# A shorter last chunk ahead of the branch, and a re-planned order of mirrored loads

## The chip, the cores and the metric

The kernel runs on one core of a Trainium2 chip. The time is device microseconds of one execution; the number that counts is the median over several runs.

## The reference

Three networks in a row, in single precision:

```python
# attention without softmax; u, v: (4, 3072, 256), z: (4, 3072, 64)
scores = (1 / S) * np.matmul(z, z.transpose(0, 2, 1))
x = (u * np.matmul(np.maximum(scores, 0.0) ** 2, v)).reshape(B * S, D)
# mixture of 8 experts with 384 slots each; x[i] goes to expert argmax(x[i] @ w_gate)
# in the order of i while that expert has slots left; later tokens are dropped
h = np.maximum(np.einsum('ecd,edf->ecf', disp, w1), 0.0)   # (8, 384, 1024)
y = np.einsum('ecf,efd->ecd', h, w2)                       # (8, 384, 256)
out[i] = gate_w[i] * y[expert_idx[i], pos[i]]   # gate_w: softmax weight; 0 where dropped
# feed-forward with ELU: 256 -> 2048 -> 256; w_in and w_out are float64
result = elu(out @ w_in) @ w_out
```

Only tokens that got a slot have an output that isn't zero. Once all 8 x 384 slots are full, the attention of all later tokens is not needed.

## The kernel before, in words

**Stages.** The kernel computes the attention of the first 3456 tokens (all of batch 0 and 384 queries of batch 1), then reads the count of the least used expert (`need`) and branches. If every expert has its 384 slots full, it goes on to the experts at once (`experts(FIRST)`); else it computes further chunks of queries until they are (`attention("later")`, not executed with these inputs). The experts run one after another, each with its 16 steps of the feed-forward network interleaved with the preparation of the next expert, with an order written out by hand (`feed_forward`).

**Attention.** The queries are cut into chunks: six of 512 (chunks 0 to 5, batch 0) and one of 384 (chunk 6, batch 1). A chunk has 24 steps, one for each tile of 128 keys. A plain step has a score (two matmuls of 128 keys by the chunk's queries, L620), a ReLU and a square on ScalarE (L1085, L1091), a rounded part (the cast, on ScalarE at L113 or VectorE at L923), the remainder on VectorE (L116), and the attend (six matmuls, L124 to L127). So numbers of single precision go through TensorE as a rounded part and a remainder, in three products.

**Mirrored steps.** Scores of batch 0 are symmetric. Where a later chunk needs a block that an earlier one computed, the earlier one stores it to DRAM (`m_store`, L653), and the later one loads it (`m_load`, four DMAs, L659) and transposes it on VectorE (L1072), in place of score, ReLU and square. `MC` says for how many tiles of each pair (row of keys, chunk) this is done: 39 steps, in chunks 1 to 5.

**Routing.** After a chunk's last attend, `route` multiplies by u (the gates, L694), forms tokens as rows with the logits beside them (matmuls, L708; copies, L720 and L722), and computes expert, position and gate weight with some 25 small VectorE operations. Then each tile of 128 tokens is scaled (L895 or L897) and scattered to `disp` in DRAM by an indirect DMA that GpSimd issues (L903). The order of the experts is set from the counts after chunk 5 (`first_expert`): the fullest one is the first, its weights are loaded, and once chunk 5 is scattered its rows are loaded (SP, L162), transposed on TensorE (L217) and split. The routing of chunk 6 itself (`trail`) runs beside the first expert.

**The order of the work.** A planner at build time (`Conductor`) places the instructions of the attention stage on TensorE, ScalarE, VectorE and SP, with modelled durations. TensorE's scores and attends have a fixed order (items). Every other job has an item for which it is needed and a `tail`, how long before it; the job whose due time is earliest goes first. A `gate` holds a job back until an item is reached; `after` names what it waits for, with extra time if given as a pair. On SP, the planner counts a backlog of DMA traffic (`dma`). The plan is then run as it is: each engine's queue is in order.

**Buffers.** The squares and the mirrored blocks live in 11 plain buffers (`own`); rounded parts and remainders in 7 (`ownr`) and in ten that are borrowed from the second network's weights until chunk 6.

**Other work in the stage.** `narrowing` turns the float64 weights into pairs of single precision on VectorE: eight loads of 1 MB, one every 14 steps from step 8 on. `fills` writes zeros to the output. `keys` and `values` load and split z and v.

## Time and profile before

| what | value |
|---|---|
| runs shown | 724.52, 725.9 and 1425.81 us, median 725.9 |
| the profiled execution | 723.64 us, its span 721.4 us |
| TensorE busy | 706.7 us of the span |
| VectorE, ScalarE busy | 569.5 us, 575.6 us |
| attention stage, to the first matmul of the first expert | 0 to 304.25 us |
| mean granted TensorE clock | 0.997 |

The times of the table are those of the chip; a row of the profile is from one execution. In what follows, TensorE is PE (its weight loads PEld), VectorE is DVE, ScalarE is ACT, GpSimd is POOL, and SP is the engine that issues most DMAs (SPq its queue). L620 is line 620 of the kernel before. The span begins at the first instruction.

### The profile page before, as it was taken

What the parts mean: (1) busy time and instruction counts of PE and PEld (TensorE: products, weight loads), DVE (VectorE), ACT (ScalarE), POOL (GpSimd) and SP (SyncE); (2) the same over time, 40 slices, a digit from 0 to 9 for tenths busy, and PEclk for the clock granted to TensorE, in tenths of its full rate; (3) what the DMA queues carried; (4) which work ended last, traced back from release to release, by engine and by line L of the source; (5) the groups of instructions that cost most, each with busy time, mean ns of one, the idle gap of its engine ahead of it and who ended that gap; (6) DMA issues with size and microseconds to landing.
All of it is one profiled execution on the core that took longest, in us unless ns stands there. A gap on an engine that the chain in (4) does not pass through costs nothing. (4 is left out here: it accounts for less than half of the span.)

```text
span 721.4 us, 11551 instructions
## 1 busy us (share of the span) xinstructions
PE 706.7 (98%) x3756; PEld 638.2 (88%) x3756; DVE 569.5 (79%) x1217; ACT 575.6 (80%) x1191; POOL 67.9 (9%) x108
## 2 busy tenths in 40 slices
PE   8999999999999999999999999999999999999996
PEld 5888888887888889998989999999999999999995
DVE  7879799788997989678867777777777777787782
ACT  7999988887897899749767777777787777787891
POOL 1003200220002200220001001001001001001011
PEclk9999999999999999999999999999999999999998
DMA  6967968799888969638440600801704405200000
GB/s 167 269 199 204 244 148 192 174 202 221 175 145 211 187 200 282 240 125 246 177 126 16 205 8 23 225 1 35 215 1 127 122 8 167 97 1 22 1 23 22
DMA packets 197856, 98.36 MB, mean 136 GB/s; under 512 B 145894, under 2 KB 188428, under 8 KB 197280
## 3 DMA queue, kind: packets, MB, share of 16 engines
q1 hardware_dynamic: 195344, 91.10, 48.3%
q0 software_dynamic: 2448, 6.49, 2.5%
q8 instruction: 30, 0.49, 0.3%
q14 instruction: 34, 0.28, 0.1%
HBM read 58.37 MB, written 38.10 MB: 134 GB/s over the span
## 5 line engine op out<-in xcount | busy, mean ns | idle before, releaser
L1689 PE MATMUL o<-wout,gh 128*128 128x512 f32 x384 | 139.3, 394 | 0.0
L1664 DVE SCALAR_TENSOR_TENSOR t<-x,t 128x384 f32<-128x384 f32 x128 | 71.4, 558 | 83.8 <-ACT t L1661 82.5
L1659 ACT ACTIVATE m<-h 128x384 f32<-128x384 f32 x128 | 62.7, 490 | 68.6 <-PE h L127 68.3
L1693 PE MATMUL o<-wout,gl 128*128 128x256 f32 x384 | 107.2, 280 | 0.2 <-DVE gl L116 0.2
L1085 ACT ACTIVATE own<-s 128x512 f32<-128x512 f32 (+1 forms) x129 | 73.3, 569 | 24.8 <-PE s L620 22.4
L124 PE MATMUL h<-xh,win 128*128 128x384 f32 x256 | 86.2, 337 | 0.5 <-DVE g L1667 0.3
L125 PE MATMUL h<-xh,win 128*128 128x384 f32 x256 | 85.6, 334 | 0.0
L1689 PEld LDWEIGHTS o<-wout,gh 128*128 128x128 f32 x384 | 71.9, 188 | 11.1
L1091 ACT ACTIVATE own<-own 128x512 f32<-128x512 f32 (+1 forms) x129 | 78.4, 609 | 2.4
L1667 DVE SCALAR_TENSOR_TENSOR g<-h,t 128x384 f32<-128x384 f32 x128 | 71.3, 557 | 4.4
L1693 PEld LDWEIGHTS o<-wout,gl 128*128 128x128 f32 x384 | 72.7, 189 | 1.1 <-DVE gl L116 0.9
L1660 ACT ACTIVATE x<-m 128x384 f32<-128x384 f32 x128 | 67.3, 525 | 4.1
L116 DVE TENSOR_TENSOR gl<-g,gh 128x384 fp32r<-128x384 f32 x128 | 70.0, 547 | 0.2 <-ACT gh L113 0.2
L113 ACT ACTIVATE gh<-g 128x384 fp32r<-128x384 f32 x128 | 65.3, 510 | 1.0 <-DVE g L1667 0.9
L127 PE MATMUL h<-xl,win 128*128 128x384 f32 x256 | 65.7, 337 | 0.0
L1661 ACT ACTIVATE t<-m 128x384 f32<-128x384 f32 x128 | 65.1, 508 | 0.0
L127 PE MATMUL acc<-ownr,vs 128*128 128x512 f32 (+1 forms) x198 | 58.5, 377 | 0.0
L124 PE MATMUL acc<-ownr,vs 128*128 128x512 f32 (+1 forms) x154 | 57.7, 375 | 0.0
L125 PE MATMUL acc<-ownr,vs 128*128 128x512 f32 (+1 forms) x154 | 57.4, 372 | 0.0
L124 PEld LDWEIGHTS h<-xh,win 128*128 128x128 f32 x256 | 48.0, 188 | 6.3 <-DVE g L1667 1.2
L620 PE MATMUL s<-zs 128*128 128x512 f32 (+1 forms) x129 | 50.3, 390 | 0.2 <-ACT row L722 0.2
L1708 POOL DMA_INDIRECT out_dram<-oy,toks x21 | 21.5, 1024 | 296.8 <-DVE oy L1707 265.5
(152 smaller groups left out, 1685.9 us busy)
## 6 DMA issues: line engine op xcount, KB each, us to landing
raw<-in_moe_w_dram SPq DMA_DIRECT2D x16, 1024.0 KB, 6.4
out_dram<-fill SPq DMA_DIRECT2D x32, 384.0 KB, 6.5
own<-mir SPq DMA_DIRECT2D x156, 64.0 KB, 2.9
vr<-in_v_dram SPq DMA_DIRECT2D x24, 256.0 KB, 3.6
mir<-own SPq DMA_DIRECT2D x28, 192.0 KB, 2.5
raw<-in_moe_w_in_dram SPq DMA_DIRECT2D x4, 1024.0 KB, 5.6
raw<-in_moe_w_out_dram SPq DMA_DIRECT2D x4, 1024.0 KB, 7.6
win<-win_d SPq DMA_DIRECT2D x8, 512.0 KB, 4.6
```

The lines of the kernel that those rows point to most:

```text
L113: nc.scalar.activation(out=out, in_=src, func=func)
L116: nc.vector.tensor_tensor(out=out, in0=src, in1=fp(hi), op=ALU.subtract)
L124: nc.tensor.matmul(out=ps, lhsT=hi, rhs=rh, start=first, stop=False)
L125: nc.tensor.matmul(out=ps, lhsT=lo, rhs=rh, start=False, stop=False)
L127: nc.tensor.matmul(out=ps, lhsT=hi, rhs=rl, start=False, stop=last)
L1085: nc.scalar.activation(out=s["a"][:, :nq], in_=s.pop("ps"), func=ACTF.Relu)
L1091: nc.scalar.activation(out=a, in_=a, func=ACTF.Square)
L1660: nc.scalar.activation(out=self.x, in_=self.m, func=ACTF.Exp, scale=-1.0)
L1664: nc.vector.scalar_tensor_tensor(out=self.t, in0=self.x, scalar=1.0, in1=self.t, op0=ALU.add, op1=ALU.mult)
L1667: nc.vector.scalar_tensor_tensor(out=self.g, in0=self.ps, scalar=0.0, in1=self.t, op0=ALU.max, op1=ALU.add)
L1689: both = lambda: nc.tensor.matmul(out=o, lhsT=hi[:, sl], rhs=w.rearrange("p a d -> p (a d)"), start=(f == 0), stop=(f == NF2 - 1),)
L1693: one = lambda: nc.tensor.matmul(out=o[:, 0:D], lhsT=lo[:, sl], rhs=w[:, 0, :], start=False, stop=False)
```

## The change

- The last chunk ahead of the branch has 320 queries (`QB`), not 384. Of its three tiles of tokens the last has 64 rows (`part`); the rows left over are zeroed. 384 stays the size of later chunks and of the zero fills (`QC`). With these inputs the least used expert, which has 384 slots, gets 386 of the first 3392 tokens (393 of the first 3456).
- Two mirrored steps fewer (`MC`): 37, not 39.
- Planner: a mirrored load may be placed 20 items ahead (17 before) and is due 11 us before its use (8 before); its transpose is planned 2.5 us after the load, that of u 2 us after its load; jobs on SP that are needed for an item are held back while the planned backlog is over 4 us.
- Narrowing starts a load every 11 steps, not 14.
- The assumed arrival of loads at the start is 7.6 and 9.1 us for the third and fourth key load (7.2 and 8.2 before) and 8.5 us for the fourth value load (8.2 before).

```diff
-    QA, QB = 512, 384
+    QA, QB, QC = 512, 320, 384
...
-            if e == "SP" and x.need is None:
-                t = max(t, self.dma - 0.5)
+            if e == "SP":
+                t = max(t, self.dma - (0.5 if x.need is None else 4.0))
...
-    FIRST, NZ = S + QB, QB
+    FIRST, NZ = S + QB, QC
+    NZERO = -(-FIRST // NZ)
...
-        MC = {(0, 1): 3, (0, 2): 4, (1, 2): 3, (0, 3): 3, (1, 3): 3, (2, 3): 3, (0, 4): 3, (1, 4): 3, (2, 4): 2, (3, 4): 2, (0, 5): 2, (1, 5): 2, (2, 5): 2, (3, 5): 2, (4, 5): 2}
+        MC = {(0, 1): 3, (0, 2): 4, (1, 2): 3, (0, 3): 3, (1, 3): 3, (2, 3): 2, (0, 4): 3, (1, 4): 2, (2, 4): 2, (3, 4): 2, (0, 5): 2, (1, 5): 2, (2, 5): 2, (3, 5): 2, (4, 5): 2}
...
-            n = nq // P
-            t0 = (b * S + q0) // P
+            n, t0 = -(-nq // P), b * S + q0
+            part = [min(P, nq - j * P) for j in range(n)]
...
+                        if part[-1] < P:
+                            nc.gpsimd.memset(t["row"][part[-1]:P, n - 1, :], 0.0)
...
+            if part[-1] < P:
+                chain("oh", lambda: nc.vector.memset(t["oh"][part[-1]:P, n - 1, :], 0.0))
...
-            LEAD, AHEAD = (3 if more else 2), 17
+            LEAD, AHEAD = (3 if more else 2), 20
...
-                        "SP", 4 * sync(nq), None, need=a_item, tail=8.0, gate=max(0, a_item - AHEAD),
+                        "SP", 4 * sync(nq), None, need=a_item, tail=11.0, gate=max(0, a_item - AHEAD),
...
-                    before(w, load)
+                    before(w, (load, 2.5))
...
-                    b, 0, {g: Begun(5.2 + g, zr=zl[g]) for g in (2, 3)},
+                    b, 0, {g: Begun(4.6 + 1.5 * g, zr=zl[g]) for g in (2, 3)},
...
-                values(b, 0, {n: Begun((5.0, 5.9, 6.8, 8.2)[n], vr=vl[n]) for n in range(4)}, {})
+                values(b, 0, {n: Begun((5.0, 5.9, 6.8, 8.5)[n], vr=vl[n]) for n in range(4)}, {})
...
-                    t = add("DVE", dve_turn(nq), None, after=[x], need=end, tail=0.9)
+                    t = add("DVE", dve_turn(nq), None, after=[(x, 2.0)], need=end, tail=0.9)
...
-            W, EVERY = 512, 14
+            W, EVERY = 512, 11
...
-            for i in range(FIRST // NZ):
+            for i in range(NZERO):
```

The rest of the diff cuts operands of the last tile to 64 rows and adapts the chunks after the branch.

## Rows read from the trace of the kernel before

**Rows 1.** The page: busy us of each engine, share of the span, instructions.
```profile
PE 706.7 (98%) x3756; PEld 638.2 (88%) x3756; DVE 569.5 (79%) x1217; ACT 575.6 (80%) x1191; POOL 67.9 (9%) x108
```

**Rows 2.** Waits, whole span: engine, line, what it waited for: total us, times, longest.
```profile
DVE own L1072 <- DMA own<-mir: 2.6, 4, 0.7
...
PE acc L127 <- DVE win L116: 0.9, 3, 0.4
```

**Rows 3.** Timeline, TensorE: start us, us, engine, line; steps in chunks 3 and 6.
```profile
149.98 0.39 PE L620 MATMUL s<-zs 128*128 128x512 f32 x1
151.80 0.39 PE L620 MATMUL s<-zs 128*128 128x512 f32 x1
...
285.85 0.33 PE L620 MATMUL s<-zs 128*128 128x384 f32 x1
...
287.24 0.33 PE L620 MATMUL s<-zs 128*128 128x384 f32 x1
```

**Rows 4.** Timeline, TensorE and its weight loads, near the end.
```profile
713.36 0.42 PEld L1693 LDWEIGHTS o<-wout,gl 128*128 128x128 f32 x2
713.59 0.40 PE L1693 MATMUL o<-wout,gl 128*128 128x256 f32 x2
...
713.82 0.39 PE L1689 MATMUL o<-wout,gh 128*128 128x512 f32 x1
```

**Rows 5.** Busy us in stretches: us, each engine (instructions), granted clock, DMA share, GB/s.
```profile
140.00:180.00 40.00, 39.08 (x179) 31.56 (x179) 34.85 (x79) 31.69 (x59) 5.06 (x9) 1.00 0.88 201
...
268.30:290.90 22.60, 22.60 (x141) 22.41 (x140) 20.69 (x69) 21.23 (x48) 0.79 (x5) 1.00 0.95 286
290.90:301.40 10.50, 10.02 (x58) 9.70 (x56) 7.88 (x16) 9.17 (x20) 4.47 (x4) 1.00 0.67 224
```

**Rows 6.** Groups by shape, whole span: count, busy us, mean ns, idle before.
```profile
L1091 ACT ACTIVATE own<-own 128x512 f32<-128x512 f32 x105 | 65.9, 629 | 1.9
...
L1091 ACT ACTIVATE own<-own 128x384 f32<-128x384 f32 x24 | 12.5, 522 | 0.5
...
L116 DVE TENSOR_TENSOR ownr<-own,ownr 128x512 fp32r<-128x512 f32 x28 | 19.2, 685 | 4.5 <-ACT ownr L113 4.3
...
L116 DVE TENSOR_TENSOR ownr<-own,ownr 128x384 fp32r<-128x384 f32 x24 | 13.3, 556 | 3.6 <-ACT ownr L113 2.1 <-ACT row L722 0.7
```

**Rows 7.** The same view, VectorE, 268.3 to 290.9: remainders and casts of chunk 6.
```profile
L116 DVE TENSOR_TENSOR ownr<-own,ownr 128x384 fp32r<-128x384 f32 x14 | 7.7, 553 | 0.9 <-ACT row L722 0.7
...
L923 DVE CAST ownr<-own 128x384 fp32r<-128x384 f32 x7 | 2.5, 359 | 0.3 <-ACT own L1091 0.2
```

**Rows 8.** Timelines of four engines: from chunk 5's gates to the first expert.
```profile
268.36 0.68 DVE L694 SCALAR_TENSOR_TENSOR ur<-acc,ur 128x512 f32<-128x512 f32 x1
...
290.66 1.34 POOL L903 DMA_INDIRECT disp<-row,idx  x1 [16.28 <-DVE row L897]
...
297.66 0.37 SPq L162 DMA_DIRECT2D rows<-disp  x1
...
301.43 0.87 PE L217 MATMUL dps<-ident,rows 128*128 128x128 f32 x6 [0.51 <-DMA rows<-disp]
...
304.25 0.34 PE L124 MATMUL h<-dh,w1hl 128*128 128x384 f32 x1
```

**Rows 9.** Timelines of TensorE and VectorE at the start.
```profile
8.86 0.50 PE L571 MATMUL zps<-identr,t 128*128 128x128 f32 x4 [1.03 <-DVE t L116]
...
9.28 0.29 DVE L1149 CAST t<-zr 128x256 fp32r<-128x256 f32 x1 [0.56 <-DMA zr<-in_z_dram]
9.49 0.68 DVE L116 TENSOR_TENSOR ownr<-own,ownr 128x512 fp32r<-128x512 f32 x1
```

**Rows 10.** The page, DMA issues: queue, count, KB each, median us to landing.
```profile
own<-mir SPq DMA_DIRECT2D x156, 64.0 KB, 2.9
```

More of the change, by code (lines that the diff above doesn't have):

```diff
@@ L59, in tile_attn_moe_ffn @@
     CT = cap // P
-    QA, QB = 512, 384
-    assert D == 256 and E == 8 and DQ == 64 and cap % P == 0 and S % QA == 0 and S % QB == 0
+    QA, QB, QC = 512, 320, 384
+    assert D == 256 and E == 8 and DQ == 64 and cap % P == 0 and S % QA == 0
     cscale = (1.0 / S) ** 2
@@ L708, in turn_x @@
                         nc.tensor.matmul(
-                            out=t["xps", j][:, d * RH:(d + 1) * RH],
-                            lhsT=us[c][:, d, j * P:(j + 1) * P], rhs=iw[:, d, :],
+                            out=t["xps", j][0:part[j], d * RH:(d + 1) * RH],
+                            lhsT=us[c][:, d, j * P:j * P + part[j]], rhs=iw[:, d, :],
                             start=True, stop=True,
@@ L717, in copy @@
                 def copy(j=j, by_dve=by_dve):
-                    ps = t.pop(("xps", j))
+                    ps, to = t.pop(("xps", j))[0:part[j], :], t["row"][0:part[j], j, :]
                     if by_dve:
-                        nc.vector.tensor_copy(out=t["row"][:, j, :], in_=ps)
+                        nc.vector.tensor_copy(out=to, in_=ps)
                     else:
-                        nc.scalar.activation(out=t["row"][:, j, :], in_=ps, func=ACTF.Copy)
+                        nc.scalar.activation(out=to, in_=ps, func=ACTF.Copy)
                 y = put("copy", "DVE" if by_dve else "ACT", 0.36, [x], 8, cost=1.0)(copy)
@@ L891, in scaled @@
                 def scaled(j=j):
-                    row, g = t["row"], t["g"]
-                    r = row[:, j, 0:TOK]
+                    q = part[j]
+                    row, g = t["row"][0:q, j, :], t["g"][0:q, j, :]
+                    r, at = row[:, 0:TOK], row[:, TOK:TOK + 1].bitcast(I32)
                     if scales[j].ran == "ACT":
-                        nc.scalar.activation(out=r, in_=r, func=ACTF.Copy, scale=g[:, j, :])
+                        nc.scalar.activation(out=r, in_=r, func=ACTF.Copy, scale=g)
                     else:
                         nc.vector.tensor_scalar(
-                            out=r, in0=r, scalar1=g[:, j, :], scalar2=None, op0=ALU.mult
+                            out=r, in0=r, scalar1=g, scalar2=None, op0=ALU.mult
                         )
-                    nc.gpsimd.tensor_copy(
-                        out=row[:, j, TOK:TOK + 1].bitcast(I32), in_=tok[:, t0 + j:t0 + j + 1]
-                    )
+                    if t0 % P:
+                        nc.gpsimd.iota(at, pattern=[[0, 1]], base=t0 + j * P, channel_multiplier=1)
+                    else:
+                        nc.gpsimd.tensor_copy(out=at, in_=tok[0:q, t0 // P + j:t0 // P + j + 1])
                     put = nc.gpsimd.indirect_dma_start(
                         out=disp[:, :],
-                        out_offset=bass.IndirectOffsetOnAxis(ap=t["idx"][:, j, :], axis=0),
-                        in_=row[:, j, :],
+                        out_offset=bass.IndirectOffsetOnAxis(ap=t["idx"][0:q, j, :], axis=0),
+                        in_=row,
                         in_offset=None,
@@ L1561, in first_flow @@
                         ps = layer1(0, f)
-                        go_on((QB // P, 2, 0)[f] if f < 3 else 1)
+                        go_on((-(-QB // P), 2, 0)[f] if f < 3 else 1)
                         hidden(0, f, ps)
@@ L1598, in later_flow @@
         def later_flow():
-            later = [(b, q, QB) for b in range(1, B) for q in range(0, S, QB)][1:]
+            odd = (S - QB) % QC + QC
+            later = [(1, QB, odd)] + [
+                (b, q, QC) for b in range(1, B) for q in range((QB + odd) * (b == 1), S, QC)
+            ]
+            assert odd <= QA and odd % SQ == 0
             with ExitStack() as ifs:
@@ L1747, in feed_forward @@
             for z in range(4):
-                i = reach // NZ + 4 * (n - 1) + z
+                i = -(-reach // NZ) + 4 * (n - 1) + z
                 if i < NTOK // NZ:
@@ L1829, in tile_attn_moe_ffn @@
     with tc.If(told[0] > 0, preferred_fallthrough_block=True, label="usual") as seldom:
-        for i in range(FIRST // NZ, NTOK // NZ):
+        for i in range(NZERO, NTOK // NZ):
             zero(i)
```

## The prediction

> **What bounds the kernel now.** I read the busy times of the page first. TensorE is busy nearly all of the span, VectorE and ScalarE about four fifths each [rows 1]. So time is either TensorE's work or one of its few gaps, and I went on to the waits for those gaps [rows 2], then to the timeline for what one step costs [rows 3, 4], and last to the stretch this change is about, the last chunk ahead of the branch, "chunk 6" (batch 1, 384 queries, 24 steps). It runs from the gates of chunk 5 at 268.4 to the first matmul of the first expert at 304.25 [rows 8]. The table of windows shows what an average over the span hides: in 268.3 to 290.9 TensorE is busy throughout, but so are ScalarE (21.2 of 22.6 us) and VectorE (20.7 of 22.6) [rows 5]. Three engines are full there at once.
>
> There is a second thing to see in that stretch. The first expert's rows are gathered from what chunk 5 routed. The chain is: gates of chunk 5 (268.36), routing on VectorE in small pieces, four indirect stores on GpSimd (first at 290.66), the load of the rows on SP (297.66), transposes on TensorE (301.43, after an idle 0.51), then the expert's first layer (304.25) [rows 8]. At 301.43 TensorE had already waited for the rows, and it had only two attend steps left. So two paths end together: TensorE's own work, and the routing chain of chunk 5. Only the first gets shorter with fewer queries.
>
> **The change part by part.**
>
> *Fewer queries.* A step of 512 queries takes 151.80 - 149.98 = 1.82 us, one of 384 takes 287.24 - 285.85 = 1.39 us [rows 3]. Both have eight matmuls, so 128 columns are worth 0.43 us a step and 64 columns 0.215. Over 24 steps TensorE saves 24 x 0.215 = 5.2 us. The three 128-row tiles of routing become two and a half, with the same instructions.
>
> Could a matmul of 320 columns be held up by its weight load? The matmul would have 0.147 us, a recorded weight load lasts 0.19, and TensorE's load row is full in chunk 6 (22.4 of 22.6 us) [rows 5]. But at the end two matmuls of 256 columns, each with its own load, start at 713.59 and within the next 0.23 us, before 713.82 [rows 4]: about 0.115 each. I count the whole 5.2; the other end is 0. The Trainium skill (Perfetto Trace Analysis, Identifying the Most-Contended Engine) judges TensorE's headroom by the busy share of its weight loads. By that the loads are the limit in chunk 6 and the saving would be nothing; the rows of 256 columns speak against it.
>
> *The other engines in chunk 6.* A square on ScalarE goes from 629 ns (512) to 522 (384), so 64 columns less save about 53 ns, 10%; the remainder on VectorE from 685 to 556, so 65 ns, 12% [rows 6]. TensorE's step shrinks by 15%. The fixed part of each instruction doesn't shrink. The same skill page (Optimizing Scalar/DVE Operations) says so and puts the fixed part at about 60 ns for VectorE and 93 for ScalarE from SBUF. The straight line through the rows gives more, about 170 and 200; the rows decide.
>
> What does that do to the routing chain? In its 22.6 us VectorE did 14 remainders and 7 casts for chunk 6 [rows 7], which are due earlier and go first, and the routing got what was left. With a step 15% shorter, 2.6 more remainders and 1.3 more casts come due in that time. At 0.49 and about 0.31 us (a cast of 384 took 0.359) that is 2.6 x 0.49 + 1.3 x 0.31 = 1.7 us more. The 14 remainders, 7 casts and 2 transposes of u that were there get about 14 x 0.065 + 7 x 0.045 + 2 x 0.065 = 1.4 us less. So the chain gets no faster, but about 0.3 us slower. ScalarE, with 1.4 us idle in that time, can't take more off VectorE. I take +0.3, with ends of -0.5 (neighbours overlap, so what is added costs less than it lasts) and +1.0 (two more casts move to VectorE). The stores, the row load and its landing (290.66 to 301.43) do not depend on the number of queries: 0.
>
> *Two mirrored steps less.* A mirrored step has six matmuls and not eight, so two score pairs return: 2 x 1.82 x 2/8 = +0.91 us on TensorE. VectorE loses two transposes and ScalarE gains four activations of about 0.6 us [rows 6] in chunks 3 and 4, where it idles 8.3 of 40 us [rows 5]: 0, and 2.4 if it were full.
>
> *More reserve behind the mirrored loads* (gate 20 items ahead, not 17; due 11 us before use, not 8; 2.5 us more between load and transpose in the plan; needed transfers held back while the planned backlog is over 4 us). VectorE waited four times for such loads, 2.6 us in all, and TensorE three times behind that, 0.9 us in all [rows 2]. That is all there is to win: -0.9, with 0 as the other end. What is late next in those places is nothing that the waits show.
>
> *Start.* The plan now thinks the third and fourth key loads later. TensorE's longest gap there is before the transposes at 8.86 (1.03 us), and the first remainder starts at 9.49 only because a key cast that waited for its load stands before it on VectorE, from 9.28 [rows 9]. Put the attend first and 0 to 0.9 us goes; I take -0.5.
>
> *Narrowing every 11 steps, not 14.* The eight 1 MB loads, with their 32 stores, come up to 21 steps earlier on SP, ahead of mirrored loads. Their VectorE work fills leftover time and nothing in chunk 6 waits for it. I take 0; if the cover goes, it appears as the slower rival below.
>
> *The rest.* Nine zero fills as before, the same three stores, one more memset on GpSimd and one on VectorE during the first expert, where VectorE waits: 0.
>
> **The sum.** Chunk 5 ends 0.91 - 0.9 - 0.5 = 0.5 us earlier. The rows land 0.3 - 0.5 = 0.2 earlier, at 301.2. TensorE's own steps would be done by 304.25 - 0.5 - 5.2 - 0.5 (the idle before the transposes) = 298.0, so it waits some 3 us for the rows. From the rows to the first layer there are the transposes and one ScalarE part, 1.2 us, if all attend steps went before, or up to 2.4 if the plan still leaves two behind the transposes as now. I take 1.5: 302.7 in place of 304.25, that is -1.5 us. From there on the work is the same. The profiled execution took 723.6, of which 721.4 is the span; it becomes 722.1. The undisturbed runs shown took 724.5 and 725.9, 0.9 and 2.3 more; I take the nearer and forecast **723.0**.
>
> **The rivals.**
>
> *TensorE bound to the end.* The routing chain gets done earlier after all, because the plan orders VectorE anew: the work of the second half of chunk 6 is lighter (7.9 of 10.5 us on VectorE [rows 5]), and jobs that are due later stand between the links of the chain now. Then the gain is 5.2 + 0.5 (the idle) + 0.9 + 0.5 - 0.9 = 6.2 at most, 718.3, and 3 to 5.5 if part of it comes: 719 to 721.5.
>
> *Chunk 6 no shorter.* The weight loads, or ScalarE, hold a step at 1.39. Then only 0.5 remains: 724. For weight loads see above. For ScalarE, it would have to stall TensorE by over 3 us before it counts, since that much is spent waiting for rows anyway.
>
> *Slower: the reserve runs out of buffers.* A mirrored load holds one of 11 plain buffers from its issue until its remainder is done; it lands 2.9 us after issue [rows 10] and will now be issued about 3 us earlier, so it holds one some 3 us longer. Narrowing takes the same buffers and now falls into the same chunks. When none is free a ReLU waits, then its attend step. For it, 10 of the 37 mirrored steps are in chunk 5 and 17 in chunks 3 and 4; against it, a plain step holds a buffer for only some two steps, and the planner counts buffers. At 0.2 us for each of those 27 steps it costs 5.4, less the 1.5: 728.4; at half of that 725.7. It decides from 1.5 us of new stalls.
>
> *The branch is taken.* From the reference's inputs the least used expert has 386 tokens among the first 3392, and the limit is 384 (393 among 3456). Two tokens of margin; if they went, at least one more chunk would follow (chunk 6 takes 36 us now), with the keys and values of its batch loaded and split again: above 758.
>
> *Not what it says* (no plan changes, gains within the noise) is covered by the second rival.
>
> **How the numbers follow.** Forecast (gain of 0.5 to 3 us) 0.43; TensorE bound 0.26; chunk 6 no shorter 0.11; buffers run out 0.18; branch 0.01; others 0.01. The likeliest's own range is 721.5 to 724. With the cases of both signs the range is 718.5 to 727.5, which leaves out about the outer half of the second and fourth. A measurement of this kernel tells about 2% (14.5 us) from no change, and no case but the branch, or a plan gone badly wrong, reaches that: faster 0.01, same 0.96, slower 0.03.
>
> **What would show it.** Right: steps of chunk 6 at about 1.17 us on TensorE; the first indirect store of chunk 5 still some 22 us after its gates; an idle of 2 to 4 us on TensorE before the transposes of the first rows; no wait of a transpose for a mirrored load; the first attend step about 0.5 us earlier. Wrong: rows landing 3 us earlier than now, so that no idle is there; steps still at 1.39; or waits of attend steps on remainders in chunks 2 to 5. If TensorE's wait for the rows let the clock fall (it is 1.00 there now [rows 5]), the first layer would start at half its pace, and I should be too low by about as much as that lasts.

## The result and the profile after

The changed kernel took 719.82 us (median of five runs, 718.7 to 720.24), the kernel before beside it 725.9 (median). One of the five runs of the kernel before took 1425.81 us; it counts in that median (725.2 without it) and not in the ratio. The ratio is 0.9919, with a 95% interval of 0.9899 to 0.994: 5.9 us less by it, well under what could count as more than no change (14.5 us), but clear of zero. The forecast was 723.0 with a range of 718.5 to 727.5. So the range held, but only because it reached down into the cases of a rival: the forecast's own case (721.5 to 724) did not come. The time lies 3.2 us below the forecast, for a reason that the forecast had priced at nothing.

The two profiled executions differ by less: 723.64 and 719.82, spans of 721.4 and 718.0. The profile of before was one of that kernel's quickest runs: beside the experiments it ran 68 times, from 723.65 to 732.16 us, with medians of 727.4, 728.31 and 727.69 on three chips. Those of its runs that took under 725.1 us had a mean granted clock of 0.996 to 0.998, and ten of the eleven above 730.4 one of 0.992 to 0.995. So a row by row account of the two traces has 3.4 us to explain, and the rest of the 5.9 is a spread of the kernel before that its one profile does not show.

In the rows below, lines stand 1 to 11 further on than before (L620 is now L621, the gates L695, the indirect stores L910, the cast L930, the mirrored transpose L1079). First the busy times of the page, which answer to [rows 1].

```profile
PE 703.5 (98%) x3760; PEld 636.1 (89%) x3760; DVE 568.6 (79%) x1222; ACT 572.9 (80%) x1189; POOL 71.9 (10%) x109
```

Nothing new can be seen there: 3 us less on TensorE, the same on the others. The waits of TensorE up to 310 us (what waited for what: us in total, times, longest) say more. They answer to [rows 2].

```profile
PE pp L807 <- DVE dl L801: 1.7, 1, 1.7
PE warm L1545 <- DVE own L1539: 1.3, 1, 1.3
PE dps L217 <- DMA rows<-disp: 0.9, 1, 0.9
PE xps L711 <- DVE ur L695: 0.8, 1, 0.8
PE zps L572 <- DVE t L116: 0.2, 1, 0.2
```

The three waits of attend steps behind mirrored loads (0.9 us) are gone. The wait for the first expert's rows is 0.9, where 0.5 was before and some 3 were forecast. Two waits are new, xps and pp: matmuls of the routing of chunk 6. Next, the timelines of four engines, from chunk 5's gates to the first expert. They answer to [rows 3] and [rows 8].

```profile
267.26 0.69 DVE L695 SCALAR_TENSOR_TENSOR ur<-acc,ur 128x512 f32<-128x512 f32 x1 [0.71 <-PE acc L127]
...
286.22 1.28 POOL L910 DMA_INDIRECT disp<-row,idx  x1 [13.31 <-DVE row L903]
...
290.40 0.31 PE L621 MATMUL s<-zs 128*128 128x320 f32 x1
...
291.58 0.31 PE L621 MATMUL s<-zs 128*128 128x320 f32 x1
...
293.04 0.37 SPq L162 DMA_DIRECT2D rows<-disp  x1
...
296.72 0.87 PE L217 MATMUL dps<-ident,rows 128*128 128x128 f32 x6 [0.88 <-DMA rows<-disp]
...
299.31 0.90 PE L711 MATMUL xps<-iw,ur 128*128 128x136 f32 x4 [0.83 <-DVE ur L695]
299.95 0.43 PE L124 MATMUL h<-dh,w1hl 128*128 128x384 f32 x1
...
305.28 0.18 PE L807 MATMUL pp<-co,ones 128*128 128x32 bf16 x1 [1.71 <-DVE dl L801]
```

A step of 320 queries lasts 291.58 - 290.40 = 1.18 us. From the gates to the first indirect store it is now 286.22 - 267.26 = 19.0 us, where it was 290.66 - 268.36 = 22.3 [rows 8]. That is the surprise of this case. The first expert starts at 299.95, 4.3 us earlier; from there to the end it takes 718.0 - 299.95 = 418.05 us, 0.9 more than before, with the pp wait of 1.7 us in it. 4.3 - 0.9 = 3.4, which is the whole difference of the spans.

Busy times in stretches (us, each engine with its instructions, granted clock, DMA share, GB/s), which answer to [rows 5]: chunk 3's, the routing of chunk 5, what follows it up to the rows, and 300 to 310.

```profile
140.00:180.00 40.00, 40.00 (x187) 33.31 (x186) 36.60 (x83) 34.35 (x65) 6.44 (x9) 1.00 0.89 212
267.20:286.20 19.00, 19.00 (x136) 18.86 (x135) 16.96 (x64) 17.76 (x45) 0.55 (x4) 1.00 0.84 259
286.20:296.70 10.50, 9.64 (x66) 9.38 (x64) 7.57 (x17) 8.59 (x21) 4.86 (x5) 1.00 0.66 210
...
300.00:310.00 10.00, 8.29 (x51) 7.68 (x50) 6.23 (x28) 4.49 (x11) 0.42 (x3) 1.00 0.01 2
```

VectorE is busy for 16.96 of 19.0 us in the routing: 89%, where it was 92%. What it did there for others is in its groups by shape in 267.26 to 286.22 (count, busy us, mean ns, idle before), which answer to [rows 7]:

```profile
L116 DVE TENSOR_TENSOR ownr<-own,ownr 128x320 fp32r<-128x320 f32 x14 | 6.8, 486 | 0.4 <-ACT ownr L113 0.2
L116 DVE TENSOR_TENSOR vs<-vr,vs 128x512 fp32r<-128x512 f32 x4 | 2.7, 687 | 0.0
L930 DVE CAST ownr<-own 128x320 fp32r<-128x320 f32 x5 | 1.6, 321 | 0.0
```

The 14 remainders of chunk 6 are still there, each 67 ns shorter (0.9 us in all); casts are 5, not the 7 of [rows 7] (6 of them up to the first store). The middle row is what the prediction passed over: remainders of the values of batch 1, 4 of them. Before, in 268.36 to 290.66, there were six:

```profile
L116 DVE TENSOR_TENSOR vs<-vr,vs 128x512 fp32r<-128x512 f32 x6 | 4.1, 684 | 0.0
```

The last VectorE operation of the narrowing tells why fewer are left (duration min/median/max, first and last start; the kernel before, then the change):

```profile
L1394 DVE SCALAR_TENSOR_TENSOR own<-own,own x16: 655/686/693, 51.9 to 257.7; 128x512 f32<-128x512 f32 x16
L1401 DVE SCALAR_TENSOR_TENSOR own<-own,own x16: 650/684/691, 51.1 to 203.9; 128x512 f32<-128x512 f32 x16
```

Before, it ran to 257.7 us, ten us short of the routing. Now it is done at 204, and splits of batch 1's values that used to come after it are done in chunk 5.

### The profile page after: what moved, and what is told of

Its sections match the earlier page's. It is cut to its first block, busy times and chain, and to the rows that moved or that the text cites. A ratio compares the mean times of both kernels' runs of the same rounds, so it can differ in the third digit from the quotient of the medians.

```text
span 718.0 us, 11564 instructions
## 1 busy us (share of the span) xinstructions
PE 703.5 (98%) x3760; PEld 636.1 (89%) x3760; DVE 568.6 (79%) x1222; ACT 572.9 (80%) x1189; POOL 71.9 (10%) x109
## 5 line engine op out<-in xcount | busy, mean ns | idle before, releaser
L1092 ACT ACTIVATE own<-s 128x512 f32<-128x512 f32 (+1 forms) x131 | 73.3, 560 | 23.1 <-PE s L621 22.2
L124 PE MATMUL acc<-ownr,vs 128*128 128x512 f32 (+1 forms) x146 | 53.0, 366 | 0.0
L125 PE MATMUL acc<-ownr,vs 128*128 128x512 f32 (+1 forms) x146 | 52.6, 363 | 0.0
L127 PE MATMUL acc<-ownr,vs 128*128 128x512 f32 (+1 forms) x180 | 51.6, 368 | 0.0
L621 PE MATMUL s<-zs 128*128 128x512 f32 (+1 forms) x131 | 51.3, 391 | 0.0
L1719 POOL DMA_INDIRECT out_dram<-oy,toks x21 | 21.1, 1003 | 297.2 <-DVE oy L1718 265.3
```

Of the source, the lines that this page charges most:

```text
L124: nc.tensor.matmul(out=ps, lhsT=hi, rhs=rh, start=first, stop=False)
L125: nc.tensor.matmul(out=ps, lhsT=lo, rhs=rh, start=False, stop=False)
L127: nc.tensor.matmul(out=ps, lhsT=hi, rhs=rl, start=False, stop=last)
L1092: nc.scalar.activation(out=s["a"][:, :nq], in_=s.pop("ps"), func=ACTF.Relu)
```

## Experiments

Four theories were to be told apart. *Narrowing*: the routing got shorter because narrowing ends earlier. *Reserve*: it is the reserve behind mirrored loads. *Casts*: it is what the plan leaves on VectorE for chunk 6. *Rows*: a long wait for the rows costs more than its own length. The expectations of e1 to e3 call the first of them N and set a rival Q beside it: shorter remainders and casts of 320 columns. Two side questions are what 320 queries are worth, and what the new waits cost. Each kernel is an edit of the changed one. e1 to e4 ran on one chip, e5 to e9 on a second, e10 to e13 on a third, each group beside its own runs of the kernel before (medians 727.4, 728.31 and 727.69); the ratios are to these and not to 725.9, and they are not quite the ratios of the medians. Since the kernel before spreads so widely, a ratio from one chip against one from another is uncertain by some 3 us. "Routing" is from the gates of chunk 5 to the first indirect store, "rows" TensorE's wait for the first expert's rows, both in the profiled execution (us).

| kernel | median us | ratio to before (95%) | routing | rows | clock in 300 to 310 |
|---|---|---|---|---|---|
| before | 725.9 | 1 | 22.3 | 0.5 | 1.00 |
| the change | 719.82 | 0.9919 (0.9899 to 0.994) | 19.0 | 0.9 | 1.00 |
| e1: 320 queries alone | 728.76 | 1.0017 (0.9993 to 1.0041) | 22.2 | 2.6 | 0.66 |
| e2: e1 and narrowing every 11 | 729.02 | 1.0017 (0.9989 to 1.0045) | 21.2 | 1.3 | 0.87 |
| e3: the change, narrowing every 14 | 725.63 | 0.9981 (0.9957 to 1.0006) | 22.5 | 3.1 | 0.66 |
| e4: the change, other place for chunk 6's routing | 716.43 | 0.9864 (0.9827 to 0.9902) | 19.0 | 0.8 | 1.00 |
| e5: the change with 384 queries | 720.57 | 0.9908 (0.9863 to 0.9953) | 21.1 | 0.4 | 1.00 |
| e6: the change without the reserve | 724.98 | 0.9967 (0.9947 to 0.9987) | 21.8 | 2.5 | 0.66 |
| e8: e4, rows from elsewhere | 715.75 | 0.985 (0.981 to 0.9889) | | 0 | 1.00 |
| e9: e3, rows from elsewhere | 722.33 | 0.9935 (0.9906 to 0.9963) | | 0 | 0.78 |
| e10: e6, casts of chunk 6 on ScalarE | 725.52 | 0.9962 (0.9935 to 0.9989) | 21.7 | 2.7 | 0.66 |
| e11: the change, casts of chunk 6 on VectorE | 722.15 | 0.9903 (0.9874 to 0.9933) | 20.1 | 0 | 0.83 |
| e12: e4, values of batch 1 sooner | 716.65 | 0.9851 (0.979 to 0.9912) | 17.7 | 0 | 1.00 |
| e13: e4 with 39 mirrored steps | 719.96 | 0.9893 (0.9831 to 0.9955) | 21.7 | 2.4 | 0.69 |

### Fewer queries alone (e1)

All other parts are undone:

```diff
-            W, EVERY = 512, 11
+            W, EVERY = 512, 14
-        MC = {..., (2, 3): 2, ..., (1, 4): 2, ...}
+        MC = {..., (2, 3): 3, ..., (1, 4): 3, ...}
-            if e == "SP":
-                t = max(t, self.dma - (0.5 if x.need is None else 4.0))
+            if e == "SP" and x.need is None:
+                t = max(t, self.dma - 0.5)
-            LEAD, AHEAD = (3 if more else 2), 20
+            LEAD, AHEAD = (3 if more else 2), 17
-   ... tail=11.0 ...   before(w, (load, 2.5))   after=[(x, 2.0)]
+   ... tail=8.0 ...    before(w, load)          after=[x]
```

(and the old times of the first loads). What 320 queries bring with them stays: the half tile and its fills.

> The smaller last chunk alone: 320 queries, with the planner's settings, the 39 mirrored steps and the narrowing every 14 steps of before. Theory N (narrowing out of the way of chunks 5 and 6 is what shortened chunk 5's routing from 22.3 to 19.0 us, gates to first indirect store): here it stays at 21.5 to 23 us, TensorE waits 2 to 4 us for the first expert's rows, and the time is 0 to 2.5 us below before. Theory Q (shorter remainders and casts of 320 columns shortened it): 19 to 20 us, and 3 to 5 us below before. Both: TensorE still waits some 0.9 us behind mirrored loads in chunk 3.

It gained nothing: 1.0017. Its waits of TensorE up to 310 us:

```profile
PE dps L217 <- DMA rows<-disp: 2.6, 1, 2.6
...
PE xps L711 <- DVE ur L695: 1.6, 1, 1.6
PE acc L127 <- DVE win L116: 1.3, 3, 0.7
```

The stretch from 300:

```profile
300.00:310.00 10.00, 6.18 (x25) 5.33 (x26) 2.31 (x5) 1.42 (x4) 0.00 (x0) 0.66 0.61 228
```

This is the picture that the prediction drew: TensorE is done with its steps, the routing chain is as long as before (22.2 us), and TensorE stands for 2.6 us. What it mentioned only as a risk happened too. After that wait the granted clock falls to 0.66 over 300 to 310: part of the time at the lower of its two levels, 1.2 and not 2.4 GHz. The 5.2 us that TensorE saved are eaten by the wait, the clock, the xps wait behind it, and a chunk 5 whose gates come at 269.9, 1.5 us later than before. Theory N has its routing and its wait; its time, 0 to 2.5 us below before, is missed or just touched (the interval of the ratio is 0.9993 to 1.0041). Theory Q is out: shorter operations alone don't shorten the routing.

### Narrowing every 11 steps, without the rest (e2)

e1 with `EVERY = 11`.

> 320 queries and narrowing every 11 steps, nothing else of the change. Theory N: narrowing ends some 40 to 50 us earlier than before, routing takes 18.5 to 20 us, and the time is 2 to 4 us below that of 320 queries alone. Theory Q: within 0.7 us of 320 queries alone.

No gain either: the time is e1's, as theory Q had it. The routing has 4 remainders of values in it as the narrowing theory wants, but it is 21.2 us, 1.0 less than in e1, where 18.5 to 20 was expected. So narrowing alone takes 1.0 of the 3.3 us. The gates of chunk 5 come 6.4 us later than before, at 274.77. The longest of VectorE's waits up to 310 us:

```profile
DVE own L1079 <- DMA own<-mir: 6.9, 6, 2.4
```

The longest of TensorE's:

```profile
PE s L621 <- ACT row L725: 3.3, 1, 3.3
```

And the two stretches about it:

```profile
190.00:195.00 5.00, 2.31 (x6) 1.83 (x7) 4.03 (x9) 2.80 (x7) 0.10 (x1) 0.64 0.78 204
195.00:200.00 5.00, 5.00 (x17) 3.98 (x16) 3.66 (x11) 3.11 (x6) 0.84 (x4) 0.68 0.78 184
```


Narrowing's loads come 11 steps apart, not 14, and so more of them fall among the mirrored loads, which come late now: 6.9 us of waits, where before had 2.6 [rows 2]. One of them stops TensorE for 3.3 us: the transpose at 190.97 waited 2.4 us for its load, a cast on ScalarE for the transpose, and the row copies behind that cast held up the next score. The clock is at 0.64 and 0.68 for the ten us around it. So narrowing every 11 steps isn't free with 39 mirrored steps and no reserve (for which of the two helps, see e6 and e13).

### The change with narrowing every 14 steps (e3)

```diff
-            W, EVERY = 512, 11
+            W, EVERY = 512, 14
```

> The changed kernel with narrowing put back to every 14 steps. Theory N: narrowing ends in chunk 5 again (after 245 us), routing takes 21.5 to 23 us, the rows land about 3 us later, and the time is 2 to 3.5 us above the changed kernel. Theory Q: routing stays at 19 to 20 us and the time within 0.7 us of the changed kernel.

The ratio is 0.9981, against 0.9919 for the whole change, and the intervals don't meet. Narrowing ends late again, the routing takes 22.5 us, and TensorE waits 3.1 us for the rows. The last operation of narrowing:

```profile
L1401 DVE SCALAR_TENSOR_TENSOR own<-own,own x16: 644/682/692, 49.8 to 257.4; 128x512 f32<-128x512 f32 x16
```

Two of VectorE's groups in the routing (267.26 to 289.82):

```profile
L116 DVE TENSOR_TENSOR vs<-vr,vs 128x512 fp32r<-128x512 f32 x6 | 4.1, 681 | 0.0
L930 DVE CAST ownr<-own 128x320 fp32r<-128x320 f32 x9 | 2.9, 317 | 0.7 <-ACT own L1098 0.7
```

The stretch from 300:

```profile
300.00:310.00 10.00, 7.11 (x30) 6.07 (x30) 3.75 (x12) 2.91 (x7) 0.42 (x3) 0.66 0.37 150
```

Six remainders of values, as before. With everything else of the change in place, the one number takes most of the gain with it, more than the 2 to 3.5 us that theory N had. So the early end of narrowing is needed for the short routing; e2 shows that it is not enough. The routing is 3.5 us longer. In it stand two remainders of values (4.1 - 2.7 = 1.4 us) and four casts of chunk 6 (2.9 - 1.6 = 1.3 us) more on VectorE, and three remainders of chunk 6 that come due in the longer time (17 in place of 14, 8.2 - 6.8 = 1.4 us). A cast of values and two operations on keys add 1.1 us; two scalings of rows less (0.5 us), one on ScalarE and one behind the first store, go off. The values and keys are what narrowing moved; that the casts moved with it is the plan's doing, and is not shown step by step.

### The change without the reserve (e6)

The reserve lines of e1's diff alone, with 320 queries, 37 mirrored steps and narrowing every 11 steps kept.

> The changed kernel with the planner's treatment of mirrored loads of before: placed up to 17 items ahead, due 8 us before use, no extra time ahead of the transposes (nor of those of u), and needed transfers not held back by the backlog. Theory C (narrowing every 11 steps puts its DMA traffic among the mirrored loads, and only the reserve keeps them in time): transposes wait 3 us or more in all for mirrored loads, TensorE waits 2 us or more behind them in chunks 3 to 5, and the time is 4 to 10 us above the changed kernel. Rival (the two mirrored steps less were what removed the waits): no such wait of TensorE over 0.5 us, and within 1.5 us of the changed kernel.

Neither side had it whole. The rival has the waits right: those for mirrored loads come to 1.0 us and stop TensorE nowhere, so with two mirrored steps fewer the loads are in time without the reserve too. It has the time wrong: the routing takes 21.8 us and the ratio is 0.9967. The waits of TensorE are those of e1 again:

```profile
PE dps L217 <- DMA rows<-disp: 2.5, 1, 2.5
PE xps L711 <- DVE ur L695: 1.6, 1, 1.6
```

And so is the stretch from 300:

```profile
300.00:310.00 10.00, 7.35 (x30) 6.19 (x30) 3.81 (x13) 3.06 (x7) 0.42 (x3) 0.66 0.08 31
```

There are 4 remainders of values in the routing, as in the change, but 9 casts of chunk 6, not 5. So the reserve pays less by the stalls that it is made for than by the plan that comes out with it in chunk 6.

### Where chunk 6's casts are done (e10, e11)

In e10, e6 with the casts of chunk 6's first 16 steps on ScalarE alone; in e11, the change with every other one of them on VectorE alone.

```diff
-   {"ACT": act(nq), "DVE": dve_copy(nq)}, None, None, need=a_item, tail=0.9,
+   {"ACT": act(nq)} if more and c == last and k < 16                    # e10
+   {"DVE": dve_copy(nq)} if more and c == last and k < 16 and k % 2     # e11
+   else {"ACT": act(nq), "DVE": dve_copy(nq)}, None, None, need=a_item, tail=0.9,
```

> The changed kernel without the reserve (e6), in which the casts of the first 16 steps of chunk 6 may only run on ScalarE. Theory V (the length of chunk 5's routing is set by how many casts and value remainders the plan puts on VectorE between its links; e6 had nine such casts, the changed kernel five): routing shortens from 21.8 to 19.5 to 20.5 us, TensorE's wait for the rows from 2.5 to about 1 us or less, the clock stays up, and the time is 2 to 5 us below e6. Rival U (ScalarE is as full as VectorE, and the casts come late there): routing is shorter, but TensorE waits as long for casts, and the time is within 1 us of e6 or above it.

> The changed kernel with the casts of every other one of the first 16 steps of chunk 6 on VectorE alone, so that at least eight run there in the routing, not five. Theory V: routing lengthens from 19.0 to 20 to 21.5 us, the wait for the rows from 0.9 to 2 us or more, and the time is 1 to 4 us above the changed kernel. Rival U: ScalarE gets that much lighter, routing stays within 0.5 us of 19.0, and the time within 0.7 us of the changed kernel.

In e11 eleven casts of chunk 6 stand in the routing, and it is 20.1 us, 1.1 longer, as the casts theory has it at its low end; but TensorE doesn't wait for the rows at all, where 2 us or more was expected. Its time can't be told from the change's: the median is 2.3 us above, the ratio 0.0016 below. e10 went against the theory: one cast of chunk 6 is left on VectorE in the routing, and it is 21.7 us, as in e6. So the number of casts is a mark of the plan and not its cause. The timelines of VectorE show where the links of the chain lie, counted from the gates. The link "need" comes at 12.0 us in the change, at 15.6 in e6, at 12.4 in e10; in e10 the 3 us are lost later, between the slots (`idx`, 283.80) and the first link of the gate weight (286.98). The plan loses about as much in both, at different places. Why it does so is open.

### What the wait for the rows costs (e8, e9)

In both, the first expert's rows are loaded from u and not from `disp`, so that they wait for no routing; this leaves out the first expert's dependence on the routing, and that expert's output is other than the reference's.

```diff
-                in_=disp.rearrange("(e t p) r -> e t p r", e=E, p=P)[
+                in_=u.rearrange("b s d -> (b s d)")[0:NSLOT * ROW].rearrange(
+                    "(e t p r) -> e t p r", e=E, p=P, r=ROW
+                )[
...
-                    after=[x, (ctx["routed", last - 1], 4.0)], load=moved(3 * P, 1088))
+                    after=[x], load=moved(3 * P, 1088))
```

> The kernel with the trail put right (e4), with the first expert's rows loaded from the input u, which is there from the start, and not from the routed tokens; its token numbers come from a constant. So the output of the first expert is another, and nothing waits for the routing of chunk 5. Theory P (once the routing is quick, TensorE is bound to the end of chunk 6 by its own work but for the 0.8 us it still waits for the rows): 0.5 to 1.5 us below e4. Theory S (something else starts the first expert, its weights or the split of its rows): within 0.4 us of e4.

> The changed kernel with narrowing every 14 steps (e3), and with the first expert's rows loaded from the input u as in e8, so that nothing waits for chunk 5's routing; the output of the first expert is another. Theory W (in e3 the wait of 3.1 us for the rows, and the clock of TensorE at half for some microseconds behind it, are what ate the gain): the wait goes, the granted clock stays 1.00 in 290 to 310, and the time is 4.5 to 7 us below e3, at or below the changed kernel. Rival (the clock falls for another reason, the gates and small operations of the last routing): the wait goes, but the granted clock still falls, and the time is 2.5 to 3.5 us below e3.

Off e4, which waits 0.8 us for the rows, this takes 0.7 us by the medians and 1.0 by the ratios: about the wait, but less than the uncertainty. The traces bear it out: from the gates of chunk 5 to the first layer it is 30.0 us in e8 and 31.0 in e4. Off e3, which waits 3.1, it takes 3.3. Theory W, that the clock would come back with the wait and 4.5 to 7 us be gained, misses the gain, and in the profiled execution the lower clock stays. e9's waits of TensorE (two lines further on than in the change):

```profile
PE pp L809 <- DVE dl L803: 1.7, 1, 1.7
PE acc L124 <- ACT ownr L113: 1.7, 1, 1.7
PE xps L713 <- DVE ur L697: 1.6, 1, 1.6
```

And its stretches about the first layer:

```profile
290.00:300.00 10.00, 8.05 (x46) 6.99 (x44) 4.29 (x8) 5.76 (x15) 3.21 (x4) 0.88 0.88 338
300.00:310.00 10.00, 7.01 (x34) 6.41 (x35) 5.16 (x19) 2.51 (x7) 0.42 (x3) 0.78 0.01 2
```

xps and pp are there as in e3, where pp comes only at 311; the wait of an attend step for its rounded part (until 295.69) is new. The clock falls at 297.5, behind this wait and ahead of the xps wait. But this execution is not the usual one: six of e9's ten have a mean granted clock of 0.998, where all twelve of e3 have 0.993 to 0.995. So without the wait for the rows the clock mostly stayed up. These six took 720.1 to 723.94 us, median 721.9, which is 3.7 below e3: more than the wait, less than theory W wanted.

### The new waits, and a faster kernel (e4, e12)

While the first expert runs, the routing of chunk 6 is called in pieces (`go_on`). A piece ends where its modelled work goes over 0.45 us. The gates of 384 queries are over that, so each of the two was a piece, and `go_on(ND)` ahead of the first layer made both. Those of 320 queries are modelled at 0.40, so both fit one piece, and the second piece is the first matmuls for the logits: TensorE waits for the gates in front of the first layer (xps, 0.8 us), and everything in `trail` is one place early, up to pp (1.7 us). In e4:

```diff
-                go_on(ND)
+                go_on(1)
                 for f in range(NF1):
-   chain("oh", lambda: nc.vector.memset(t["oh"][part[-1]:P, n - 1, :], 0.0))
+   chain("oh", lambda: nc.vector.memset(t["oh"][part[-1]:P, n - 1, :], 0.0), pace=0.0)
```

> The changed kernel, with the routing of the last chunk begun by one step (its two gates) and not two ahead of the first expert's first layer, so that its first logit matmuls stand behind that layer and not ahead of it, and the new small memset not counted when the routing is spread. Theory T (TensorE's two new waits there, 0.8 us for the gates and 1.7 us for the routing's small operations, are an accident of how the shorter operations are counted): both go, and the time is 1.5 to 2.5 us below the changed kernel. Rival: the first layer or the next operations wait as long in their place, and the time is within 0.5 us.

Its waits of TensorE up to 310 us:

```profile
PE warm L1545 <- DVE own L1539: 1.3, 1, 1.3
PE dps L217 <- DMA rows<-disp: 0.8, 1, 0.8
PE zps L572 <- DVE t L116: 0.6, 2, 0.5
```

And its timeline, TensorE:

```profile
295.64 0.88 PE L217 MATMUL dps<-ident,rows 128*128 128x128 f32 x6 [0.81 <-DMA rows<-disp]
297.23 0.34 PE L124 MATMUL h<-dh,w1hl 128*128 128x384 f32 x1
...
298.27 1.92 PE L711 MATMUL xps<-iw,ur 128*128 128x136 f32 x12
```

Both waits are gone. From the transposes to the first layer it is 1.6 us, not 3.2, and the logits stand behind the first layer. It takes 716.43 us (715.81 to 717.64, where the change has 718.7 to 720.24), 0.9864: quicker than both kernels, though the two ratios' intervals just meet. That is 3.4 us by the medians, where 1.5 to 2.5 was expected. The spans differ by 3.9: 1.1 were gained before the transposes (1.0 of it at the start of the kernel, which the last section takes up), 1.6 between them and the first layer, and 1.2 behind it.

e12 adds an earlier start of the values of batch 1:

```diff
-   0, where["s", (c, 0)] - 22 + 4 * n
+   0, where["s", (c, 0)] - 30 + 4 * n
```

> The kernel with the trail put right (e4), with the loads of the values of batch 1 let go eight items earlier. Theory V: fewer than four value remainders fall into chunk 5's routing, which takes under 18.5 us, and the remaining wait of 0.8 us for the rows goes: 0.5 to 1.2 us below e4. Rival: the values can't be split earlier, since the steps of chunk 5 still read the tiles they replace, or they push chunk 5's own work: within 0.4 us of e4 or above it.

The routing is 17.7 us, and the rows are there before TensorE wants them. But the time is 716.65, the same as e4's: what could still be had was 0.8 us, and the intervals are wider than that. In its routing stand 2 remainders of values, not 4, which is 1.3 of the 1.3 us that it is shorter. So it bears out one half of the narrowing theory from the other side: values sooner, routing shorter.

### 384 queries, and 39 mirrored steps (e5, e13)

```diff
-    QA, QB, QC = 512, 320, 384
+    QA, QB, QC = 512, 384, 384                    # e5: the change
...
-        MC = {..., (2, 3): 2, ..., (1, 4): 2, ...}
+        MC = {..., (2, 3): 3, ..., (1, 4): 3, ...}    # e13: e4
```

> The changed kernel with 384 queries in the last chunk again; the planner's settings, 37 mirrored steps and narrowing every 11 steps stay. Theory N (narrowing out of the way makes the routing quick enough for the shorter chunk): routing takes about 19 to 20 us here too, the rows land some 3 us before TensorE needs them, TensorE is busy to the first expert, and the time is 3 to 5 us above the changed kernel and 0 to 2.5 us below the kernel before. Theory R (the reserve alone brings the gain): within 1 us of the changed kernel.

> The kernel with the trail put right (e4), with 39 mirrored steps. By the price of a score pair on TensorE (0.455 us each) it is 0.9 us below e4, if the reserve alone keeps the loads in time. Rival (two steps less were needed too): VectorE's or ScalarE's plan gets tighter, a wait for mirrored loads or a longer routing comes back, and it is at or above e4.

Theory N's prices are missed: the routing is 21.1 us and the time only 0.75 us above the change. Theory R's price is met, but e6 shows that the reserve alone is not the reason either. With 384 queries the rest of the change gives 0.9908, as much as all of it, within the intervals: the 5 us that 320 queries take off TensorE's work bring 0.75 us by the medians and nothing by the ratios. e5's first layer starts at 303.57, 3.6 us later than the change's, but it has neither an xps wait nor a pp wait. With these waits out of the way (e4) 320 queries show in part: 716.43 against 720.57, or 3.2 us by the ratios, whose intervals still meet.

Two mirrored steps more in e4 should have saved TensorE 0.9 us by the prediction's price. They cost 3.5 by the medians (2.1 by the ratios), as the rival had it. Mirrored loads come late again (VectorE waits 1.4 us for them), so chunk 3's gates come late too, and TensorE waits for these at 184.97 (the xps row below, nearly all of its 1.45 us idle in 180 to 220). The routing of chunk 5 is 21.7 us, and TensorE waits for the rows:

```profile
PE dps L217 <- DMA rows<-disp: 2.4, 1, 2.4
PE xps L711 <- DVE ur L695: 1.4, 1, 1.4
```

## Why the prediction was right, and where it was wrong

**TensorE's own work: right.** A step of 320 queries was to be 1.17 us; it is 1.18. The weight loads, busy for 18.86 of the 19.0 us, did not hold it up. The Trainium skill (Perfetto Trace Analysis, Identifying the Most-Contended Engine) names the busy share of the weight loads as one of two measures of TensorE's headroom; by it there was none there. The trace shows there was, as [rows 4] had it. The rival in which chunk 6 gets no shorter is out.

**Mirrored loads: right in what is seen.** The 0.9 us of TensorE's waits are gone, and 140 to 180 us is full. The last attend of chunk 5 starts 0.9 us earlier, where 0.5 was said. But the start was not 0.5 earlier: the first attend came at 9.88 us, 0.7 later than before (the last section shows with what that goes). In the executions that started at full pace it came at 9.20 and 8.99 with the old start (before, e1) and at 8.87, 8.91 and 9.11 with the new (e3, e4, e9), so the term of -0.5 is worth some 0.1 on average. From the first to the last attend it is then 1.6 us less, where +0.91 and -0.9 left nothing. Waits that are gone account for 1.1 of it; why two more score pairs don't show is not worked out.

**"The routing chain gets no faster, but about 0.3 us slower": wrong, and this is the step that failed.** It got 3.3 us shorter, far outside the ends of -0.5 and +1.0. The sum behind the 0.3 counted what a shorter step does to chunk 6's own remainders and casts on VectorE, and held all else in the stretch fixed. For e1, where only the queries differ, that is right: 22.2 us in place of 22.3. The prediction's remark that neighbours on VectorE overlap is borne out as well: two gates of 0.69 us each take 1.28 us together in e2 (from 185.77), so recorded durations, and the straight line through them, overstate what one more operation costs. What it held fixed has in it 4.1 of some 16 us that VectorE does for others there: six remainders of values. They stand in the same view as [rows 7].

**"Narrowing: its VectorE work fills leftover time and nothing in chunk 6 waits for it. I take 0": wrong, the other half of the same step.** Nothing waits for narrowing, but what is due later than it gets VectorE only when it is done. Moved from 258 to 204 us, its end frees VectorE in chunk 5 for values that then don't stand in the routing. e3 shows it: the same change with 14 for 11 has a routing of 22.5 us, a wait for the rows of 3.1, and 0.9981. e12 shows the other direction for the values. How much of the 3.3 us is narrowing's depends on the rest of the plan: 3.5 in the change (e3), 1.0 without it (e1 against e2).

**"TensorE waits some 3 us for the rows": right as a mechanism, wrong for this kernel.** In e1, e3, e6, e10 and e13 it is what happens: 2.6, 3.1, 2.5, 2.7 and 2.4 us. With the forecast's routing, the change would have been one of those. And there the forecast would have been too low, as its last sentence feared: e3 takes 725.63 and e6 724.98, since the granted clock falls behind the wait and the xps wait comes on top.

**The sum.** The first layer was to start 1.5 us earlier and starts 4.3 earlier; the rest of the run was to be the same and is 0.9 longer (pp among it). So -1.5 became -3.4 in the spans. TensorE was done with its steps at 295.84, 5.1 us earlier than before, where 5.7 was said, and the rows were there at 296.72, 4.7 earlier, where 0.2 was said. That is the rival "TensorE bound to the end", all but the last 0.9 us. It was given 719 to 721.5, and its reason, that the plan orders VectorE anew, is what happened. It got a chance of no more than 0.26: the row that it named, 7.9 of 10.5 us, is of the stretch behind the routing, and what stands between the links of the chain was not looked up. That the range held is owed to this rival, not to the forecast's sum.

**The slower rival** had its place in mirrored loads and narrowing in one chunk. In the change it did not come. In e2, without the reserve, it did: 6.9 us of late loads, 3.3 us of TensorE, and the same 1.0017 as e1, so that the shorter routing brought nothing. Not because buffers run out, as the rival had it: the loads themselves come late. What keeps it away is above all the two mirrored steps given back: with 37 VectorE waits 0 to 1.2 us for mirrored loads, with or without the reserve, and TensorE nowhere behind them (the change, e3, e4, e6, e10, e11); with 39 it waits 2.6, 5.3 and 6.9 us without the reserve (before, e1, e2) and 1.4 with it (e13), and TensorE behind it each time.

**What stays open.** Narrowing every 11 steps explains two remainders of values. It does not explain why the routing takes 19.0 us with everything in place, but 21.1 to 21.8 with 384 queries, without the reserve, or with 39 mirrored steps, all of which have narrowing every 11 steps. The remainders of values are 4 in all of these, as in the change. Nor does the number of chunk 6's casts on VectorE tell it: 9 in e6 and e13, but 4 in e5, 1 in e10, and 11 in e11 with its 20.1 us. Each of these edits changes the plan of chunk 6 as a whole; no run here isolates which link is put late. Open too is why the runs of the kernel before spread over 8 us and the five of the change over 1.5: a part of it is the granted clock, and the kernels with a long wait for the rows spread too (e1 over 3.8 us, e3 over 4.5), but no profile of one of the longer runs of the kernel before was taken. It matters for the gain: e5's first layer starts only 0.7 us earlier than before, and its span is only 1.5 us shorter, and yet its ratio is the change's. So a part of the gain by the ratios lies in this spread, which the two profiles don't show.

## What to carry to other kernels

When two paths end together, shortening one brings next to nothing: e1 took 5 us of work off TensorE and gained nothing, since the chain of small operations beside it was as long as before; look first at everything that the shared engine does while that chain runs, other stages' work too, and ask what sets when that work is done. "Fills leftover time" is no price of zero under a planner: moving the end of such work moves what is planned behind it. And where code counts pieces of work by a modelled duration against a limit, a smaller size can shift the whole order behind it (e4: 3.4 us by the medians for one number and one pace).

## What the runs showed of the hardware that was not expected

**The clock falls behind a wait of a few us, but not behind each.** With a wait for the rows of 2.4 to 3.1 us the granted clock over 300 to 310 us was 0.66 to 0.69 (e1, e3, e6, e10, e13). It went to the lower level, 0.50, within 0.8 us of the end of that wait, before any further one had ended; in e13 none followed, and it was 0.73 over 299 to 300, with TensorE still idle, and 0.50 over 300 to 306. With waits for the rows of 0.9 and 0.8 us it stayed at 1.00 (the change, e4). Behind waits of 1.7 us it went either way: in e11 it stayed up behind xps and fell behind pp (0.83 over 300 to 310); in the change it stayed up behind pp. A matmul of 512 columns that is mostly recorded with 0.39 us was then recorded with 0.63, and they started 0.43 apart where 0.23 is usual (e2, from 193 us).

**At the start, matmuls may run at half pace while the granted clock reads 1.00.** In the change's profile the first scores start 0.43 us apart:

```profile
7.71 0.63 PE L621 MATMUL s<-zs 128*128 128x512 f32 x1
8.13 0.63 PE L621 MATMUL s<-zw,zs 128*128 128x512 f32 x1
...
9.88 0.57 PE L124 MATMUL acc<-ownr,vs 128*128 128x512 f32 x1
```

In e4's they are 0.23 apart, and the first attend comes 1.0 us earlier:

```profile
7.25 0.39 PE L621 MATMUL s<-zw,zs 128*128 128x512 f32 x1
7.48 0.39 PE L621 MATMUL s<-zs 128*128 128x512 f32 x1
...
8.91 0.47 PE L124 MATMUL acc<-ownr,vs 128*128 128x512 f32 x1
```

The granted clock is 1.00 over 6 to 8 us in both. Kernels with the same start are found on both sides (e3 at 8.87, e5 at 10.06 and e6 at 9.91 us), so it goes with the execution and not with the edit. A gain or loss of 1 us at the start, read from one profile, says nothing.
